# K, Q and x of a fused attention and MLP kernel turned in other ways, with the order of its work held as tables

## The chip, the cores and the metric

The kernel runs on one core of one Trainium2 chip. The metric is the time of one execution on the device in microseconds; the median of three runs is compared. A core has TensorE (PE; its weight loads are listed as PEld), VectorE (DVE), ScalarE (ACT), GpSimd (POOL) and SyncE (SP). DMAs are issued from the queues of SP, ACT and POOL and carried by 16 DMA engines.

## The reference

Causal attention in which each query sees only the best 6 of 24 chunks of 32 keys, followed by an MLP with ELU.

```python
B, H, S, D = 4, 8, 768, 64          # chunk = 32, nc = 24, top_k = 6
k_min, k_max = min and max of k over each chunk          # per head dimension
ub = sum over d of max(q * k_min, q * k_max)             # -1e9 where the chunk lies ahead
top_chunks = argsort(ub)[..., -6:]
scores = q @ k.T / sqrt(D);  scores = -1e9 outside the chosen chunks and above the diagonal
attn = softmax(scores);  o = attn @ v
x = o.transpose(0, 2, 1, 3).reshape(B * S, H * D)        # 3072 x 512
h = x @ w_in                                             # 3072 x 2048
out = where(h > 0, h, exp(min(h, 0)) - 1) @ w_out        # 3072 x 512
```

q, k and v have the shape (4, 8, 768, 64) in 32-bit floats; w_in is 512 x 2048, w_out 2048 x 512.

## The kernel before, in words

The unit of work is a pair of heads of one batch (16 pairs, `u` from 0 to 15, four to a batch), and within it a half of the 768 positions (`hf`, 384 each). The two heads of a pair lie on partitions 0 to 63 and 64 to 127.

For each pair K and Q must have the head dimension on partitions. In batches 1 to 3 (`pair_prep`, from L613) four DMAs a tensor bring K and Q in 128-byte pieces into `stage`, SP issues them (L623), and the DVE turns them in 32x32 blocks (L636, L654). In batch 0 (`first_prep`, from L670) sixteen loads of K and Q (one a pair, half and tensor; L706; the first two Qs from ACT's queue) bring four consecutive tokens of a head, 1 KB, to each of 96 partitions; they are kept in two `gT` buffers, `stage` and `kt`. V comes in sixteen DMAs (L712) in pieces of 256 bytes. TensorE turns a block (`turn`, L735): for each of the four tokens and both heads a 32-bit matmul of 96x64 against a 96x96 identity, written to a PSUM bank (psH for K, psMT for Q). Since the tokens come out in four interleaved groups, the copies that follow undo this: ScalarE's for K (L759), Q (L779) and relu(Q) (L784), and the DVE's chunk minima and maxima (L765).

Then, for two pairs together, `quad_sel` computes the chunks' bounds on TensorE (L833) and picks the best six on DVE (L850 to L873); POOL copies the result as mask rows below Q (L884). `pair_attend` computes scores (L925, triangle L931), exponentials on ScalarE (L952), the triangle on POOL (L971) and the product with V (L984); the DVE divides by the sum (L997, L1000) into `on`, 128 tokens x 3 blocks x 128 columns. TensorE turns `on` in three bf16 transposes (L1009) into a PSUM bank, ScalarE copies the bank to `xT` (L1012). This happens once for each pair and half, 32 times.

`mlp(b, hf)` multiplies the `xT` of a batch's four pairs by w_in in 16 blocks (L1034), applies ELU with ScalarE and DVE (L1044 to L1078), multiplies by w_out (L1097), copies (L1105) and stores from SP (L1109). It follows the attention of its batch by two or three pairs, so that TensorE always has dense work between the attention's steps.

The order is not written out: every operation is registered with an engine, a duration and a priority (`Plan.add`), and `Plan.order` simulates engines, DMA queues and buffers and lets each engine take the ready operation of least priority number. RANKS moves single priorities. The result is a sequence in which the operations are emitted, with a buffer slot for each tile. Each engine then executes its operations in that order.

Of the kernel before, what the change touches and what calls it, by code (L numbers as in the profile page):

```python
# [13 lines left out]
F32 = mybir.dt.float32  # L14
# [3 lines left out]
H = 8  # L18
# [24 lines left out]
def WHEN(q_in, left, out):  # L43
# [8 lines left out]
TURN = 0.7  # L52
FILL = {}
TWO = False
# [4 lines left out]
RANKS = ((0, 1, 127), (11, 1, 71), (17, 1, -43), (33, 1, -100), (37, 1, -51), (48, 1, 127), (49, 1, -12),  # L59
# [60 lines left out]


class Plan:

    LAT = {"PE": 0.21, "ACT": 0.17, "DVE": 0.13, "POOL": 0.08, "SP": 2.2, "POOLQ": 2.5}

    BEGIN = 0.85  # L130
    COLD = 7.0
    RING = 2560
    LANES = 8
# [1065 lines left out]
```

## Time and profile before

| | us |
|---|---|
| median of three runs (least, most) | 272.35 (272.06, 272.52) |
| span of the profiled execution, first to last instruction | 276.5 |
| TensorE busy in it | 266.1 (96%) |
| DVE, ScalarE, POOL busy | 198.8, 202.8, 124.5 |

No time is recorded for the profiled execution other than its span; the span is 4.15 us above the median of the runs. In the lists of instructions the columns are: start and duration (timeline) or count, busy time and mean of one (groups), the engine, the line of the kernel, the operation, the tile written and the tiles read, the form. "x16" is the number of instructions that the line stands for. Matmuls are pipelined: the distance between the starts of two neighbours is what one costs.

### The profile page before, as it was taken

What the parts mean: (1) busy time and instruction counts of PE and PEld (TensorE: products, weight loads), DVE (VectorE), ACT (ScalarE), POOL (GpSimd) and SP (SyncE); (2) the same over time, 40 slices, a digit from 0 to 9 for tenths busy, and PEclk for the clock granted to TensorE, in tenths of its full rate; (3) what the DMA queues carried; (4) which work ended last, traced back from release to release, by engine and by line L of the source; (5) the groups of instructions that cost most, each with busy time, mean ns of one, the idle gap of its engine ahead of it and who ended that gap; (6) DMA issues with size and microseconds to landing.
All of it is one profiled execution on the core that took longest, in us unless ns stands there. A gap on an engine that the chain in (4) does not pass through costs nothing.

```text
span 276.5 us, 6918 instructions
## 1 busy us (share of the span) xinstructions
PE 266.1 (96%) x2573; PEld 165.0 (60%) x2600; DVE 198.8 (72%) x526; ACT 202.8 (73%) x382; POOL 124.5 (45%) x219
## 2 busy tenths in 40 slices
PE   8889998899999999999999999999999999999995
PEld 4778855565555565655556565666556655555544
DVE  5944686995998998799699953876884846615920
ACT  2956799994797899988979989779579744435411
POOL 5783182794687499766537776010062200000000
PEclk9965899999999999999999999999999999999999
DMA  7999989499997999999974301101010111011022
GB/s 183 235 236 189 189 124 167 73 162 152 149 235 112 199 149 183 177 173 153 158 168 79 78 2 38 40 0 40 10 70 0 40 39 38 28 51 38 2 76 76
DMA packets 111473, 29.81 MB, mean 108 GB/s; under 512 B 101072, under 2 KB 108496, under 8 KB 111440
## 3 DMA queue, kind: packets, MB, share of 16 engines
q1 hardware_dynamic: 106800, 24.78, 48.2%
q0 software_dynamic: 4224, 4.19, 9.8%
q8 instruction: 20, 0.33, 0.5%
q10 hardware_dynamic: 416, 0.39, 0.5%
q14 instruction: 13, 0.11, 0.1%
HBM read 27.26 MB, written 6.29 MB: 121 GB/s over the span
## 4 chain that ended last, share of the span: by engine, by line
PE 71%; DMA 10%; DVE 5%; ACT 5%; issue 3%; SPq 2%; POOL 2%; ACTq 0%; DVEq 0%; POOLq 0%
PE psM L1097 17%; PE psH L1034 15%; PE psS L925 10%; PE psS L1034 8%; PE psMT L1097 7%; PE psO L984 6%; DMA gT<-in_q_dram 4%; DMA w_out_sb<-in_moe_w_out_dram 3%; ACT pt L952 2%; PE psS L833 2%; PE psT L1009 2%; PE psH L735 2%; DMA stage<-in_q_dram 2%; DMA stage<-in_k_dram 1%; SPq L712 1%
## 5 line engine op out<-in xcount | busy, mean ns | idle before, releaser
L952 ACT ACTIVATE pt<-psS 128x768 bf16<-128x768 f32 (+1 forms) x120 | 90.0, 788 | 9.1 <-PE psS L925 7.8
L1034 PE MATMUL psH<-xT,w_in_sb 128*128 128x384 bf16 x384 | 72.9, 325 | 0.1
L1097 PE MATMUL psM<-w_out_sb,gT 128*128 128x512 bf16 x264 | 68.2, 379 | 1.6 <-DMA w_out_sb<-in_moe_w_out_dram 0.2
L1034 PEld LDWEIGHTS <-w_in_sb 128*128 128x128 bf16 x512 | 48.2, 97 | 32.8 <-issue 0.9
L971 POOL TENSOR_SCALAR_AFFINE_SELECT pt<-pt 128x256 bf16<-128x256 bf16 (+1 forms) x56 | 28.8, 518 | 65.5 <-ACT pt L952 64.2
L925 PE MATMUL psS<-rhs,lhs 88*128 88x384 bf16 (+4 forms) x304 | 55.3, 292 | 1.6 <-ACT pt L952 0.7
L1097 PEld LDWEIGHTS <-gT 128*128 128x128 bf16 x400 | 37.1, 97 | 33.0 <-issue 1.2
L1044 ACT ACTIVATE e<-psH 128x384 f32<-128x384 f32 x96 | 47.0, 513 | 8.9 <-PE psH L1034 7.2
L925 PEld LDWEIGHTS <-lhs 88*128 88x128 bf16 x304 | 28.8, 101 | 17.0 <-issue 2.5
L984 PEld LDWEIGHTS <-pt 128*128 128x128 bf16 x672 | 28.5, 99 | 9.6 <-issue 1.7
L1073 DVE SCALAR_TENSOR_TENSOR t<-e,psH 128x384 bf16<-128x384 f32 x48 | 25.5, 545 | 12.1 <-ACT e L1044 11.9
L801 POOL CAST rhs<-qt 64x768 bf16<-64x768 f32 (+1 forms) x40 | 27.9, 701 | 13.3 <-ACT qt L779 11.5
L884 POOL COPY rhs<-selt 24x576 bf16<-24x576 bf16 (+2 forms) x40 | 22.6, 564 | 25.0 <-DVE selt L873 23.3
L984 PE MATMUL psO<-vext,pt 128*128 128x65 bf16 x672 | 32.1, 196 | 0.3 <-POOL pt L971 0.2
L1052 DVE SCALAR_TENSOR_TENSOR gT<-e,psH 128x384 bf16<-128x384 f32 x48 | 25.3, 540 | 9.7 <-ACT psH L1049 9.6
L1044 ACT ACTIVATE e<-psS 128x768 f32<-128x768 f32 x16 | 13.0, 810 | 18.4 <-PE psS L1034 18.4
L1078 DVE SCALAR_TENSOR_TENSOR gT<-psH,t 128x384 bf16<-128x384 f32 x48 | 25.5, 545 | 0.5
L1049 ACT ACTIVATE psH<-psH 128x384 f32<-128x384 f32 x48 | 24.5, 522 | 0.0
L801 POOL CAST lhs<-kt 64x768 bf16<-64x768 f32 x24 | 19.9, 831 | 6.7 <-DVE kt L636 4.5
L1034 PE MATMUL psS<-xT,w_in_sb 128*128 128x384 bf16 x128 | 22.4, 326 | 0.0
L1097 PE MATMUL psMT<-w_out_sb,gT 128*128 128x512 bf16 (+1 forms) x109 | 22.1, 348 | 0.2
L1012 ACT ACTIVATE xT<-psT 128x384 bf16<-128x384 bf16 x32 | 15.8, 501 | 8.6 <-PE psT L1009 8.5
(66 smaller groups left out, 287.6 us busy)
## 6 DMA issues: line engine op xcount, KB each, us to landing
out_dram<-osb SPq DMA_DIRECT2D x23, 256.0 KB, 2.0
stage<-in_k_dram SPq DMA_DIRECT2D x48, 96.0 KB, 3.6
stage<-in_q_dram SPq DMA_DIRECT2D x48, 96.0 KB, 3.8
vd<-in_v_dram SPq DMA_DIRECT2D x12, 384.0 KB, 4.7
w_in_sb<-in_moe_w_in_dram POOLq DMA_DIRECT2D x4, 512.0 KB, 8.4
w_out_sb<-in_moe_w_out_dram POOLq DMA_DIRECT2D x4, 512.0 KB, 9.5
gT<-in_v_dram SPq DMA_DIRECT2D x16, 96.0 KB, 5.1
gT<-in_k_dram SPq DMA_DIRECT2D x6, 192.0 KB, 5.0
```

What stands on the lines that cost most here:

```text
L801: nc.gpsimd.tensor_copy(out=o, in_=i)
L925: nc.tensor.matmul(p_s[:, hd, pc:pc + w], lhsT=tiles[pt_["kb"]][0:64 + NCH, hd, 128 * kb:128 * kb + 128], rhs=tiles[pt_["qb"]][0:64 + NCH, ...
L952: lambda bs=bs, pt=pt, wtot=wtot, lo=lo, at=at: nc.scalar.activation(out=tiles[pt][:, :, lo:lo + wtot], in_=tiles[bs[0]][:, :, at:at + wto ...
L971: nc.gpsimd.affine_select(out=a, in_=a, compare_op=AOT.is_ge, fill=0.0, base=0, pattern=pat, channel_multiplier=-1)
L984: nc.tensor.matmul(po[:, hd, qi, :], lhsT=tiles[pt][:, hd, off:off + 128], rhs=tiles[pt_["vx"]][:, 6 * hd + kb, :], start=(kb == 0), stop= ...
L1034: nc.tensor.matmul(ph, lhsT=w_in_sb[:, kk, f0:f0 + 128], rhs=tiles[XT[4 * b + kk]][:, c0:c0 + HALF], start=(kk == 0), stop=(kk == NKK - 1))
L1044: lambda e=e, view=view: nc.scalar.activation(out=tiles[e][:, 0:step], in_=view(), func=AF.Exp),
L1049: lambda view=view: nc.scalar.activation(out=view(), in_=view(), func=AF.Relu),
L1052: lambda e=e, view=view, fc=fc, gt=gt: nc.vector.scalar_tensor_tensor(out=tiles[gt][:, fc:fc + step, :], in0=tiles[e][:, 0:step], scalar=1 ...
L1073: lambda e=e, t=t, view=view: nc.vector.scalar_tensor_tensor(out=tiles[t][:, 0:step], in0=tiles[e][:, 0:step], scalar=1.0, in1=view(), op0 ...
L1078: lambda t=t, view=view, fc=fc, gt=gt: nc.vector.scalar_tensor_tensor(out=tiles[gt][:, fc:fc + step, :], in0=view(), scalar=0.0, in1=tiles ...
L1097: nc.tensor.matmul(pm, lhsT=tiles[gt][:, fc, 128 * tt:128 * tt + 128], rhs=w_out_sb[:, fc, cs], start=(fc == 0), stop=(fc == NFC - 1))
```

## The change

Four things are changed.

- **Loads of batch 0.** K and Q of four heads come in one load of three DMAs, one for each block of 128 tokens: a token to a partition, four heads of 64 numbers (256 bytes each) beside each other. There are eight such loads instead of sixteen. V of all eight heads comes in one load of three DMAs a half. All are staged in three `gT` buffers.
- **Turns of batch 0.** A block of 128 tokens by two heads (128x128, 32 bits) is turned by one `nc.tensor.transpose`; three make a turn. The tokens come out in order, so the copies and reductions read the bank straight.
- **Turns of x in batches 1 to 3.** `on` goes to `xT` by a transposing DMA issued by SP, 24 in all; the three transposes on TensorE and ScalarE's copy are not made there. Batch 0 keeps them.
- **The order.** `Plan.order` no longer simulates; it reads the operations' numbers from ORDER and the slots from SLOTS. RANKS and the constants of the simulation are gone.

```diff
+XDMA = (False, True, True, True)
-TURN = 0.7
+TURN = 0.40
+VLATE = 2.2
...
-RANKS = ((0, 1, 127), (11, 1, 71), (17, 1, -43), (33, 1, -100), (37, 1, -51), (48, 1, 127), (49, 1, -12),
...
+ORDER = (
+    0, 3, 13, 15, 6, 1, 43, 2, 4, 10, 45, 8, 7, 5, 9, 25, 11, 19, 26, 153, 12, 31, 20, 37, 28, 32, 47, 29, 21, 155,
+    33, 80, 22, 38, 59, 34, 48, 40, 23, 27, 60, 41, 17, 53, 35, 49, 24, 39, 36, 50, 61, 71, 54, 51, 81, 65, 56, 183,
...
+    1308, 1568, 1589, 1314, 1590, 1569, 1591, 1315, 1574, 1592, 1318, 1570, 1575, 1511, 1571, 1319, 1512, 1572,
+    1556, 1557, 1513, 1558, 1514, 1576, 1560, 1593, 1515, 1561, 1562, 1516, 1563, 1517, 1585, 1594, 1316, 1595,
+    1518, 1520, 1586, 1596, 1521, 1519, 1522, 1577, 1523, 1524, 1525, 1320, 1578, 1309, 1321, 1579, 1580, 1581,
+    1587, 1618, 1588, 1582, 1583, 1597, 1619, 1622, 1620, 1584, 1598, 1623, 1630, 1322, 1624, 1621, 1323, 1604,
...
     def order(self):
-        ops = self.ops
...
+        left = iter(SLOTS)
+        return [(self.ops[i], [(h, next(left)) for h in self.ops[i].alloc]) for i in ORDER]
...
+        def load(h, at, src, h0, w, eng):
             def f():
...
+                for n in range(3):
+                    eng.dma_start(out=tiles[h][:, at, n, :].rearrange("p (h d) -> p h d", d=D),
+                                  in_=src[a + P * n:a + P * n + P, h0:h0 + w])
             return f
...
+        if j == 0:
+            early = hf == 0 and g == 0
+            fetch(1.5, pl, load(sh, 2 * g, kb0, 4 * g, 4, nc.sync), [(sh, 2 * g)], (0.0185, 1536, 3), alloc=[] if g else [sh])
+            fetch(1.5, pl + 0.1, load(sh, 2 * g + 1, qb0, 4 * g, 4, nc.scalar if early else nc.sync), [(sh, 2 * g + 1)],
+                  (0.0185, 1536, 3), eng="ACT" if early else "SP")
+            if not g:
+                fetch(1.5, pl + VLATE, load(sv, hf, vb0, 0, 8, nc.sync), [(sv, hf)], (0.0185, 3072, 3), alloc=[] if hf else [sv])
...
-                for j in range(4):
-                    for hd in range(2):
-                        x0 = 256 * hd + 64 * j
-                        nc.tensor.matmul(p_[64 * hd:64 * hd + 64, 96 * j:96 * j + 96], lhsT=at()[0:96, x0:x0 + 64],
-                                         rhs=ident_f[0:96, 0:96], start=True, stop=True)
+                for n in range(3):
+                    nc.tensor.transpose(p_[:, P * n:P * n + P], tiles[sh][:, i, n, P * j:P * j + P], ident_f)
             return f
...
+            if XDMA[u // 4]:
+                uid[0] += 1
+                w = ("turned", uid[0])
+                o = add("SP", 0.5, pr,
+                        lambda on=on, hf=hf: nc.sync.dma_start_transpose(
+                            out=tiles[xt_h][:, HALF * hf:HALF * hf + HALF].rearrange("p (n t) -> p n t", n=3),
+                            in_=tiles[on].rearrange("p n h d -> p (n h d)")),
+                        reads=[on], writes=[w, (xt_h, hf)], alloc=[] if hf else [xt_h], lat=0.0)
+                add("DMA", 0.0, 0.0, lambda: None, reads=[w], writes=[(xt_h, hf)], free=[on], lat=2.0,
+                    dma=("SP", 0.03, 384, 1), issues=o)
+                return
```

The numbers in ORDER count the operations as they are registered. For the steps that are named later: 1517 to 1522 are the products with V of pair 14, second half, 1523 and 1524 the DVE's division, 1525 its transposing DMA; 1563 is that of pair 15; 1577 and 1581 are up-projections of batch 3's first half (eight matmuls each), 1320 and 1321 down-projections of batch 2 (four each); 1618 is the first up-projection of batch 3's second half.

More of the change, by code (lines that the diff above doesn't have):

```diff
@@ L187, in order @@
     def order(self):
-        ops = self.ops
-        for first, n, shift in RANKS:
-            for o in ops[first:first + n]:
-                o.prio += 0.02 * shift
-        for o in ops:
-            o.left = len(o.deps) + len(o.after)
-            o.ready = 0.0
-            o.start = o.end = None
-            for d in o.deps:
-                d.users.append(o)
-            for d in o.after:
-                d.followers.append(o)
-        free_slots = {c: [(0.0, i) for i in range(n)] for c, n in self.caps.items()}
@@ L234, in order @@
-        waiting = {}
-        for o in ops:
-            if o.eng == "DMA":
-                continue
-            waiting.setdefault(o.eng, [])
-            engines[o.eng] = self.BEGIN
-            if not o.left:
-                waiting[o.eng].append(o)
-        n_left = sum(o.eng != "DMA" for o in ops)
-        port = {"POOL": 0.0, "DVE": 0.0}
-        out = []
-        parts = {}
-        stalls = []
-        taken, asked = 2 * WARM, self.FETCH[0]
-        queues = {"SP": [], "ACT": [], "POOL": []}
@@ L739, in fill @@
-        def fill(i, bb, done):
-            n = FILL.get((u - SPLIT[0], hf, i), 0)
-            if not n:
-                return False
-            def f():
-                for _ in range(n):
-                    nc.tensor.matmul(ps(bb, [P, HALF], F32), lhsT=blank[:, 0:P], rhs=blank[:, 0:HALF], start=True, stop=True)
-            add("PE", 0.163 * n, pr - 0.01, f, reads=["blank"], writes=[done], alloc=bb, ni=2 * n)
-            return True
-        def tok(x):
-            return x.rearrange("q (j p) -> q p j", j=4)
@@ L754, in first_prep @@
[L754 to L756 removed]
+                for n in range(3):
+                    nc.tensor.transpose(p_[:, P * n:P * n + P], tiles[sh][:, i, n, P * j:P * j + P], ident_f)
+            return f
+        add("PE", TURN, pr, turn(bk, 2 * g), reads=[(sh, 2 * g), "ident"], writes=[bk[0]], alloc=bk, ni=6)
@@ L1154 @@
     steps = plan.order()
-    if DUMP is not None:
-        DUMP(steps)
     with tc.manual_schedule():
```

273 lines of the change are left out of this document (24 added, 249 removed), and 158 rows, old and new, of tables (ORDER, RANKS, SLOTS).

## The prediction

> **What bounds the kernel now.** I read the page's first two parts and the chain, to find the engine that sets the time.
>
> ```profile
> span 276.5 us, 6918 instructions
> PE 266.1 (96%) x2573; PEld 165.0 (60%) x2600; DVE 198.8 (72%) x526; ACT 202.8 (73%) x382; POOL 124.5 (45%) x219
> ...
> PEclk9965899999999999999999999999999999999999
> ...
> PE 71%; DMA 10%; DVE 5%; ACT 5%; issue 3%; SPq 2%; POOL 2%; ACTq 0%; DVEq 0%; POOLq 0%
> ```
>
> TensorE is busy for 96% of the span and carries 71% of the chain; the next engines stand at 72 and 73%. The clock row has one hole: from the third slice to the fifth (13.8 to 34.6 us) the granted clock falls. The windows show when each thing binds (columns: length, busy time of PE, PEld, DVE, ACT and POOL, then granted clock, DMA share, GB/s).
>
> ```profile
> 7.00:13.00 6.00, 5.04 (x134) 4.50 (x128) 5.55 (x13) 5.58 (x14) 4.59 (x9) 1.00 1.24 238
> 13.00:20.00 7.00, 5.98 (x97) 5.03 (x98) 4.08 (x26) 3.96 (x13) 5.84 (x13) 0.73 1.17 233
> 20.00:30.00 10.00, 10.00 (x110) 8.91 (x107) 3.71 (x10) 6.46 (x13) 3.55 (x8) 0.51 0.96 186
> ...
> 50.00:70.00 20.00, 18.96 (x213) 11.70 (x215) 17.18 (x49) 16.16 (x31) 14.67 (x24) 1.00 0.95 141
> ...
> 90.00:110.00 20.00, 19.59 (x190) 12.12 (x191) 18.77 (x44) 17.85 (x30) 15.71 (x26) 1.00 1.14 177
> 110.00:130.00 20.00, 19.83 (x177) 11.64 (x178) 18.07 (x52) 17.42 (x39) 14.07 (x22) 1.00 0.96 169
> ...
> 150.00:170.00 20.00, 19.78 (x208) 11.97 (x211) 13.62 (x44) 18.18 (x32) 16.30 (x26) 1.00 0.20 48
> ```
>
> Three stretches: a head to about 35 us, in which loads run at 230 GB/s and TensorE gets half its clock while it is 100% busy; a middle to 150 us in which both TensorE (98 to 99%) and the DMA engines (share near 1) are full; and the rest, in which the DMA share is 0.2 or less and only TensorE is full. So an instruction taken off TensorE shortens the run by its own length, as long as what feeds the next matmul keeps up. The whole idle time of TensorE is 276.5 - 266.1 = 10.4 us; there is little else to win.
>
> **Turns of x.** The change takes the turns of batches 1 to 3 off TensorE and ScalarE and gives them to SP as transposing DMAs.
>
> ```profile
> L1012 ACT ACTIVATE xT<-psT 128x384 bf16<-128x384 bf16 x32 | 15.8, 501 | 8.6 <-PE psT L1009 8.5
> ...
> L1009 PE MATMUL psT<-ident_b,on 128*128 128x128 bf16 x96 | 10.8, 222 | 0.8 <-DVE on L1000 0.8
> ```
> ```profile
> 30.10 0.33 PE L1009 MATMUL psT<-ident_b,on 128*128 128x128 bf16 x3
> 30.26 0.44 PE L984 MATMUL psO<-vext,pt 128*128 128x65 bf16 x9
> ...
> 31.59 0.34 PE L1009 MATMUL psT<-ident_b,on 128*128 128x128 bf16 x3
> 31.77 0.41 PE L984 MATMUL psO<-vext,pt 128*128 128x65 bf16 x8
> ```
>
> 96 matmuls are 32 turns of three; 24 of them go. One holds TensorE from its start to the next group's start: 0.16 and 0.18 us, so 24 x 0.17 = 4.1 us, all at full clock and nearly all in stretches where TensorE is full. I count it whole. ScalarE loses 24 x 0.50 = 12 us; at 73% it does not bind, so I count nothing for it, nor for the PSUM bank that each turn held.
>
> **Turns of K and Q.** Before, a turn is eight 32-bit matmuls, seen as 16 records; after, three 128x128 ones. There are 16 turns.
>
> ```profile
> 6.03 0.83 PE L735 MATMUL psMT<-ident_f,gT 96*64 96x96 f32 x16
> 6.69 0.83 PE L735 MATMUL psH<-ident_f,gT 96*64 96x96 f32 x16
> ...
> 21.46 1.55 PE L735 MATMUL psH<-ident_f,gT 96*64 96x96 f32 x16
> 22.94 0.29 PE L984 MATMUL psO<-vext,pt 128*128 128x65 bf16 x2
> ```
>
> Start to start, 0.66 us at full clock and 1.48 at half. No row shows a 32-bit 128x128 transpose. From below: three bf16 ones take 0.17. From above: if the two heads of a pair now overlap in the array, 768 columns in 0.66 us hide another 768, a column costs 1.72 ns alone, and 3 x 128 columns cost 0.66, no gain. I take what 384 columns cost at the row's own 0.86 ns: 0.33 us. So 16 x (0.66 - 0.33) = 5.3 us at full clock (0 to 7.8). About five turns stand in the half-clock stretch and save as much again: 5 x 0.33 = 1.65. Sum 6.9 us. The cover that this needs: TensorE must have other work ready; with 10.00 busy of 10 at 20 to 30 us it has.
>
> The copies out of PSUM change from interleaved to contiguous reads; a 64x384 copy took 483 ns and a contiguous 128x384 one 513, so nothing is counted.
>
> ```profile
> L1044 ACT ACTIVATE e<-psH 128x384 f32<-128x384 f32 x96 | 47.0, 513 | 8.9 <-PE psH L1034 7.2 <-DVE gT L1052 1.0
> L759 ACT ACTIVATE lhs<-psH 64x384 bf16<-64x384 f32 x16 | 7.7, 483 | 6.4 <-PE psH L735 6.2
> ```
>
> **Loads of batch 0.** K and Q come in eight loads of 384 KB (three DMAs each) instead of sixteen of 192 KB, in pieces of 256 bytes instead of 1 KB; V, in 256-byte pieces before too, in two loads behind the K and Q of the first heads.
>
> ```profile
> 4.79 1.41 PE L735 MATMUL psH<-ident_f,gT 96*64 96x96 f32 x16
> ...
> 8.66 0.88 PE L735 MATMUL psH<-ident_f,gT 96*64 96x96 f32 x16 [0.49 <-DMA gT<-in_k_dram]
> ```
>
> Now the first turn starts at 4.79 us, the second pair's K (the turn at 6.69) two turns later. After, the first turn needs what the first two pairs needed, so it starts near 6.7; but four turns then follow at 0.33 and end at 8.0, before the third pair's turn started at 8.66. ScalarE begins later by some 1.5 us; half of the head's cost of that is taken back by turns that come together. I take +1.0 us (0 to +3). The loads issue on SP and ACT without waits; behind them on ACT's queue stands only its table load.
>
> A rule of the Trainium skill speaks against it: "DMA: Bandwidth & Descriptors", section Specifications, gives 512 bytes as the least piece for line rate, below which a read-modify-write is made. The head's rows, with V in 256-byte pieces among the loads, hold 233 to 238 GB/s; the middle's, mostly 128-byte pieces, 141 to 177. By that rule K and Q would run like the middle; it is priced as a rival below.
>
> **The transposing DMAs.** Each moves 96 KB, waits on SP for the DVE's `on`, and behind it on SP stand the K, Q and V loads of the next pairs, for which the DVE's 32x32 transposes wait, and the stores of the output, whose buffers ScalarE's copies take next.
>
> ```profile
> out_dram<-osb SPq DMA_DIRECT2D x23, 256.0 KB, 2.0
> stage<-in_k_dram SPq DMA_DIRECT2D x48, 96.0 KB, 3.6
> ...
> stage<-in_q_dram SPq DMA_DIRECT2D x1, 192.0 KB, 9.4
> ```
> ```profile
> 244.50 0.86 PE L984 MATMUL psO<-vext,pt 128*128 128x65 bf16 x22
> 245.21 1.89 PE L1097 MATMUL psMT<-w_out_sb,gT 128*128 128x512 bf16 x7
> 246.93 0.33 PE L1009 MATMUL psT<-ident_b,on 128*128 128x128 bf16 x3
> 247.10 1.03 PE L1097 MATMUL psMT<-w_out_sb,gT 128*128 128x512 bf16 x4
> 247.96 2.76 PE L1034 MATMUL psS<-xT,w_in_sb 128*128 128x384 bf16 x16
> ```
>
> No transposing DMA is in the trace. By size the nearest row is the 96 KB load, 3.6 us; the quickest is 2.0, the slowest 9.4. When the last x falls due the DMA engines are nearly idle, so I take 3. The tightest hand-off is the last. In the new order there stand on TensorE, between the last product with V of batch 3 (entry 1522) and the first matmul that needs its x (1618), entries 1577, 1320, 1321 and 1581: two times eight matmuls of 384 columns (half of the 2.6 us that the sixteen from 247.96 occupy, 1.3 each) and two times four of 512 (0.86 each, 247.10 to 247.96), 4.3 us in all. The DVE needs about 1 us for the division, which leaves 3.3 for issue and landing. I take 0.5 us lost over all hand-offs (0 to 18, below). For batch 1 the cover is similar: scores, products with V and two groups of four down-matmuls. The DMA engines' extra 24 x 96 KB = 2.4 MB are, at 141 to 177 GB/s, 14 to 17 us of transfer; a third of it falls where their share is near 1, and K and Q of batch 2 come that much later, some 5 us. That batch's loads are asked for well ahead and DMA is idle from 150 us on; nothing counted.
>
> **The clock.** The hole, closer:
>
> ```profile
> 15.00:16.00 1.00, 0.84 (x17) 1.00 1.19 235
> 16.00:17.00 1.00, 1.00 (x26) 0.58 1.25 214
> ...
> 29.00:30.00 1.00, 1.00 (x16) 0.60 1.23 210
> 30.00:31.00 1.00, 1.00 (x37) 1.00 1.23 203
> ```
>
> From about 16.2 to 29.8 us, 13.6 us at half clock, worth 6.8 us of full-clock work. I leave it as it is: the new head has the same kind of small matmuls and the same waits around 12 to 15 us.
>
> **Sum.** -4.1 (x) - 6.9 (K and Q) + 1.0 (head) + 0.5 (hand-offs) = -9.5 us: span 276.5 to 267.0. The span of this profile is 4.15 us above the median of the runs, 272.35; I carry that difference over unchanged: **262.9 us**.
>
> **Rivals.**
> 1. The clock stays low longer. The hole opened although TensorE was then busy all the time, so it is not busy time alone that opens the gate; the new turns may count for even less. Shut from the first turn (6.7) to the first dense matmuls (34.67 before, some 32 after), 25 us instead of 13.6: up to 5.7 us more, 268.6. For it: 100% busy at 0.50 for 13 us. Against: fewer such matmuls.
>
> ```profile
> 34.67 3.42 PE L1034 MATMUL psH<-xT,w_in_sb 128*128 128x384 bf16 x20
> ```
>
> "TensorE: Matmul & The Clock Gate", Part 4, in the Trainium skill says the same: transpose mode does not count as busy time for the gate. No transpose-mode matmul with 32 bits is in this trace to agree or not.
> 2. The gate does not shut: the head's waits of 12 to 15 us vanish with the earlier turns; 6.8 us less where TensorE binds, of which 5 are felt: 257.9.
> 3. The head hangs on its loads: 3.15 MB of K and Q at 141 instead of 235 GB/s is 22.3 instead of 13.4 us, 8.9 us more, of which the gain of the turns hides some 4: about 268. Against: V's pieces did not slow the head.
> 4. The turns do not get cheaper (0.66 each): 262.9 + 6.9 = 269.8.
> 5. **Slower**: the transposing DMA lands late. At 9.4 us, the slowest row, each hand-off that has 3.3 us of cover stalls 6.1; with three such (first of batch 1, both of batch 3) 18 us, less the 0.5 counted: 280. It outweighs the gain of 10 once three stalls make 10, that is from a landing of 3.3 + 3.3 = 6.6 us. For it: SP is one ordered queue on which the turn stands among loads. Against: at the last hand-off no load is left.
> 6. The gain is eaten: stalls of the new order and DMA contention in the middle give back 8 to 11 us: 271 to 274.
>
> **Chances.** Forecast 0.46 (259 to 266), rival 1 0.12, 2 0.08, 3 0.06, 4 0.08, 5 0.13, 6 0.07. Rivals 1 to 4 and the forecast are faster: 0.80. Rival 6 is split, 0.03 within 0.2% (about what a measurement of this kernel can tell from no change) and 0.02 each side; with 5, slower 0.15, same 0.03, faster 0.82. The range takes in the forecast and rivals 1 to 4, from 256.5 to 270.5 us; outside are 5 and 6, 0.20.
>
> **What would show it.** TensorE's busy time near 256 us, still over 95% of the span; turns of three records at about 0.33 us; 24 transposes in the DMA table landing within 3 us or so; first up-projection before 34.67 us. The forecast is wrong if TensorE's idle time grows past 15 us, with waits on xT's DMA ahead of the up-projection, or if the clock row has a longer hole.

## The result and the profile after

The changed kernel takes 271.2 us (median of 20 runs, 269.7 to 272.6). Against the kernel before, run beside it on the same chip, the ratio is 0.995 with a 95% interval of [0.9933, 0.9967]: 0.5% faster, some 1.4 us, where 262.9 was forecast and 270.5 was the upper end of the range. In some executions of the kernel before, the profiled one of the prediction among them, TensorE ran at half clock for some 13 us; they take about 277.5 us instead of 272 and are left out of all ratios here. So the kernel before is shown here by a second profile, taken in the first experiment, in which the clock stayed up (execution 271.75 us, span 270.0; for the changed kernel 271.61 and 269.9).

The page of the changed kernel, and below it the same rows of the kernel before with its clock up:

```profile
span 269.9 us, 6328 instructions
PE 253.0 (94%) x2295; PEld 151.5 (56%) x2320; DVE 200.3 (74%) x526; ACT 192.0 (71%) x358; POOL 123.7 (46%) x219
...
q1 hardware_dynamic: 124800, 27.15, 59.2%
...
PE 66%; DMA 13%; DVE 9%; ACT 3%; issue 2%; SPq 2%; POOL 2%; ACTq 0%; DVEq 0%; POOLq 0%
```
```profile
span 270.0 us, 6945 instructions
PE 261.6 (97%) x2600; PEld 159.8 (59%) x2600; DVE 199.1 (74%) x526; ACT 202.6 (75%) x382; POOL 124.8 (46%) x219
...
q1 hardware_dynamic: 106800, 24.78, 49.2%
...
PE 76%; ACT 10%; DMA 4%; DVE 4%; issue 2%; POOL 2%; SPq 1%; ACTq 0%; DVEq 0%; POOLq 0%
```

By these rows TensorE's busy time fell by 8.6 us and its idle time grew from 270.0 - 261.6 = 8.4 us to 16.9. Some 1.3 us of that are a gap in the record: the changed kernel's page has 2295 matmuls beside 2320 weight loads, so 25 matmuls are missing (all down-projections), and each leaves a hole of about 0.05 us in work that ran on. So about 7.3 us came off TensorE, where 4.1 + 5.3 were forecast, its idle time is nearer 15.6 us, and the span stayed. In the chain, TensorE went from 76 to 66%, DMA from 4 to 13%. The question is why 7.3 us taken off the engine with the most work became about as much waiting. The windows show where (columns as before: length, busy time of PE, PEld, DVE, ACT, POOL, clock, DMA share, GB/s); first after, then before:

```profile
13.00:20.00 7.00, 5.34 (x95) 4.39 (x93) 5.36 (x29) 6.90 (x20) 5.78 (x13) 1.00 1.26 186
20.00:30.00 10.00, 7.64 (x129) 5.99 (x130) 8.33 (x34) 9.60 (x23) 5.70 (x12) 1.00 1.23 221
...
50.00:70.00 20.00, 17.95 (x169) 10.01 (x170) 16.22 (x45) 13.05 (x26) 12.51 (x19) 1.00 1.18 176
...
130.00:150.00 20.00, 18.64 (x170) 10.64 (x171) 19.12 (x53) 16.43 (x31) 14.22 (x23) 1.00 1.08 156
```
```profile
13.00:20.00 7.00, 6.39 (x132) 5.50 (x134) 5.13 (x28) 5.87 (x17) 6.48 (x14) 1.00 1.13 234
20.00:30.00 10.00, 9.57 (x196) 7.79 (x192) 7.65 (x33) 9.33 (x21) 4.37 (x9) 1.00 1.22 223
...
50.00:70.00 20.00, 20.00 (x195) 11.73 (x194) 17.51 (x50) 15.27 (x30) 13.43 (x21) 1.00 1.05 158
...
130.00:150.00 20.00, 20.00 (x237) 11.80 (x235) 18.37 (x54) 18.23 (x36) 13.50 (x22) 1.00 0.70 125
```

From 20 to 30 us TensorE idles 2.36 us (0.43 before), from 50 to 70 it idles 2.05 (0), from 130 to 150 1.36 (0). What it waits for is not one thing. The waits of TensorE in the changed kernel (waiting line, releaser: us in all, times, longest):

```profile
PE psS L709 <- ACT pt L736: 1.7, 3, 0.8
PE nothing L955 <- DVE blank L953: 1.3, 1, 1.3
PE psH L829 <- DMA w_in_sb<-in_moe_w_in_dram: 1.2, 1, 1.2
PE psMT L541 <- DMA gT<-in_q_dram: 1.1, 2, 0.8
PE psM L892 <- DMA w_out_sb<-in_moe_w_out_dram: 0.9, 1, 0.9
```

The wait on `blank` is there before too. The others are exponentials, the loads of Q, and both weights. Nobody on TensorE waits for a transposing DMA, though the up-projections read what they write. The rows of that DMA (the issue on SP; least, median and most) and the time from issue to landing:

```profile
L792 SPq DMA_TRANSPOSE xT<-on x24: 1178/1221/2724, 85.9 to 231.9; - x24
...
DMA to landing us min/median/max: 2.3/2.5/6.1
```

### The profile page after: what moved, and what is told of

The parts are those of the page before. It is cut to its first block, busy times and chain, and to the rows that moved or that the text cites. A ratio compares the mean times of both kernels' runs of the same rounds, so it can differ in the third digit from the quotient of the medians.

```text
span 269.9 us, 6328 instructions
## 1 busy us (share of the span) xinstructions
PE 253.0 (94%) x2295; PEld 151.5 (56%) x2320; DVE 200.3 (74%) x526; ACT 192.0 (71%) x358; POOL 123.7 (46%) x219
## 3 DMA queue, kind: packets, MB, share of 16 engines
q1 hardware_dynamic: 124800, 27.15, 59.2%
## 4 chain that ended last, share of the span: by engine, by line
PE 66%; DMA 13%; DVE 9%; ACT 3%; issue 2%; SPq 2%; POOL 2%; ACTq 0%; DVEq 0%; POOLq 0%
PE psM L892 18%; PE psH L829 17%; PE psS L709 9%; PE psS L829 8%; PE psMT L892 8%; PE psO L768 5%; DMA w_in_sb<-in_moe_w_in_dram 4%; DMA stage<-in_k_dram 3%; DMA vd<-in_v_dram 2%; DMA gT<-in_q_dram 2%; DMA stage<-in_q_dram 1%; SPq L455 1%; POOL rhs L668 1%; ACT lhs L547 1%; DVE gT L847 1%
## 5 line engine op out<-in xcount | busy, mean ns | idle before, releaser
L736 ACT ACTIVATE pt<-psS 128x768 bf16<-128x768 f32 (+2 forms) x120 | 89.1, 781 | 18.5 <-PE psS L709 16.6
L829 PE MATMUL psH<-xT,w_in_sb 128*128 128x384 bf16 x384 | 73.9, 325 | 2.8 <-DMA w_in_sb<-in_moe_w_in_dram 1.2
L829 PEld LDWEIGHTS <-w_in_sb 128*128 128x128 bf16 x512 | 47.4, 97 | 36.7 <-issue 4.0
L839 ACT ACTIVATE e<-psH 128x384 f32<-128x384 f32 x96 | 46.3, 505 | 14.5 <-PE psH L829 13.5
L709 PE MATMUL psS<-rhs,lhs 88*128 88x384 bf16 (+4 forms) x304 | 54.0, 283 | 1.8 <-ACT pt L736 1.7
L768 PEld LDWEIGHTS <-pt 128*128 128x128 bf16 x672 | 32.0, 98 | 13.9 <-ACT pt L736 1.4
L768 PE MATMUL psO<-vext,pt 128*128 128x65 bf16 x672 | 36.9, 194 | 1.6 <-DVE rc L781 0.6
L709 PEld LDWEIGHTS <-lhs 88*128 88x128 bf16 x304 | 26.8, 98 | 14.3 <-issue 2.1
L857 DVE TENSOR_SCALAR t<-e 128x768 bf16<-128x768 f32 x16 | 8.8, 558 | 16.3 <-ACT e L839 16.3
```

The lines of the kernel that those rows point to most:

```text
L709: nc.tensor.matmul(p_s[:, hd, pc:pc + w], lhsT=tiles[pt_["kb"]][0:64 + NCH, hd, 128 * kb:128 * kb + 128], rhs=tiles[pt_["qb"]][0:64 + NCH, ...
L736: lambda bs=bs, pt=pt, wtot=wtot, lo=lo, at=at: nc.scalar.activation(out=tiles[pt][:, :, lo:lo + wtot], in_=tiles[bs[0]][:, :, at:at + wto ...
L768: nc.tensor.matmul(po[:, hd, qi, :], lhsT=tiles[pt][:, hd, off:off + 128], rhs=tiles[pt_["vx"]][:, 6 * hd + kb, :], start=(kb == 0), stop= ...
L829: nc.tensor.matmul(ph, lhsT=w_in_sb[:, kk, f0:f0 + 128], rhs=tiles[XT[4 * b + kk]][:, c0:c0 + HALF], start=(kk == 0), stop=(kk == NKK - 1))
L839: lambda e=e, view=view: nc.scalar.activation(out=tiles[e][:, 0:step], in_=view(), func=AF.Exp),
```

## The experiments

The theory that the traces suggest: the turns' time was saved where TensorE was not what the next step waited for, so it turned into waiting. Its rivals: the time had worth and was eaten, by the short pieces of the loads, by ScalarE, or by an order that does not suit the operations. Ratios are to the kernel before, run beside each kernel on the same chip; where two experiments are compared, their ratios are. 0.1% is 0.27 us.

**The offset of the profile.** The prediction set its sum against a span 4.15 us above the median. The kernel before, with no edit at all:

> The kernel before, unchanged. Its 20 runs fall into two groups, about 272 and 277.5 us, and the profile that the prediction was made from (span 276.5, clock 0.974) has a hole of 13.6 us at half clock. Theory A, the hole is the second group: runs near 277.5 show a mean granted clock near 0.97 and runs near 272 one of 0.99 or more; a profile of the 272 kind has no hole and TensorE busy near 260 us instead of 266. Theory B, the two groups have another cause: the clocks of both groups are alike and a profile of the 272 kind has the hole too.

But for two (274.9 us at 1.0 and 276.1 at 0.981), the runs came in two groups: 271.65 to 273.5 us at a mean granted clock of 0.998 to 1.0, and 277.5 to 278.1 at 0.973 to 0.975; the prediction's profile has 0.974. Time is span + 1.7 in both. The offset was the clock hole, and nothing that one carries over.

**The size of the turns, and where their time has worth.** Three runs put TensorE's time back into the changed kernel, and nothing else. First the turns of batch 0 as 32-bit matmuls:

```diff
-nc.tensor.transpose(p_[:, P * n:P * n + P], tiles[sh][:, i, n, P * j:P * j + P], ident_f)
+nc.tensor.matmul(p_[:, P * n:P * n + P], lhsT=tiles[sh][:, i, n, P * j:P * j + P], rhs=ident_f,
+                 start=True, stop=True)
```

> The changed kernel with one thing undone: each 128x128 block of batch 0's K and Q is turned by a 32-bit matmul against the identity in place of the transpose (48 of them, the same order, buffers and loads). If a turn of three then costs about 0.66 us as the eight small matmuls did before, TensorE's busy time rises by 16 x 0.33 = 5.3 us. Theory H (the time that the cheaper turns save is not worth anything in this head, because the turns wait for loads and ScalarE and the next matmuls wait for w_in): 271 us, within 1.5 us of the changed kernel, and TensorE's idle time falls by about what its busy time gains. Theory W (TensorE's time is worth its full length there, and the gain was lost elsewhere): 274.5 to 277. If the turn costs 0.33 as a matmul too, neither is told and the transpose was no cheaper than the matmul.

Then the turns of x, by matmuls of zeros:

```diff
+if u >= 4 and hd == 1 and qi == 2:
+    for _ in range(5):
+        nc.tensor.matmul(po[:, hd, qi, :], lhsT=blank[:, 0:P], rhs=blank[:, 0:D + 1], start=True, stop=True)
```

> The changed kernel with TensorE's time for the turns of x put back: in pairs 4 to 15, ahead of the last product with V of each half, five matmuls of 65 columns of zeros against zeros, which the product then overwrites (24 x 5, some 0.17 us a half, 4 us in all). The transposing DMAs stay. Theory H (where the order leaves TensorE waiting, its time has no worth; the pairs of batch 1, to 110 us, wait): TensorE's idle time takes back up to half, +1.5 to +3 us. Theory W (whole worth): +4 us, 275.

Then both edits at once:

```diff
+    nc.tensor.matmul(p_[:, P * n:P * n + P], ...
...
+    for _ in range(5):
+        nc.tensor.matmul(po[:, hd, qi, :], lhsT=blank[:, 0:P], ...
```

> Both at once: the changed order, loads and transposing DMAs with TensorE's time as it was before the change (some 9 us more busy time). Theory H: 272.5 to 275. Theory W: 278 to 281. If the two single runs add up here, the stretches do not touch each other.

| | TensorE busy, us | span | ratio to before |
|---|---|---|---|
| changed kernel | 253.0 (25 records missing; some 254.3 with them) | 269.9 | 0.9950 [0.9933, 0.9967] |
| + K and Q time | 258.0 | 268.7 | 0.9935 [0.9897, 0.9972] |
| + x time | 257.0 | 270.0 | 0.9989 [0.9961, 1.0017] |
| + both | 262.0 | 272.6 | 1.0056 [1.0016, 1.0097] |

The rows of the turns, as matmuls and as transposes (start and duration; the distance of two starts is what a turn costs):

```profile
13.00 0.94 PE L541 MATMUL psMT<-ident_f,gT 128*128 128x128 f32 x6
13.77 0.83 PE L541 MATMUL psH<-ident_f,gT 128*128 128x128 f32 x6
14.44 0.25 PE L710 MATMUL psS<-rhs,lhs 88*128 88x192 bf16 x1
```
```profile
8.21 0.85 PE L541 MATMUL psMT<-ident_f,gT 128*128 128x128 f32 x3
8.85 0.85 PE L541 MATMUL psH<-ident_f,gT 128*128 128x128 f32 x3
9.49 0.37 PE L709 MATMUL psS<-rhs,lhs 88*128 88x192 bf16 x1
...
14.84 0.52 PE L541 MATMUL psH<-ident_f,gT 128*128 128x128 f32 x3
15.19 0.82 PE L541 MATMUL psMT<-ident_f,gT 128*128 128x128 f32 x6
```

A turn by matmuls costs 0.67 us (13.77 to 14.44), by transposes 0.35 (14.84 to 15.19) once the first ones, at 0.64, are past: the 0.33 of the prediction was nearly right for twelve of the sixteen. Sixteen at 0.67 make 10.7 us, twelve at 0.35 and four at 0.64 make 6.8, so the head saves some 3.9 us by it. They have no worth that can be seen: with them put back the kernel is no slower (0.9935 beside 0.9950; by the two intervals, at most about 0.7 us slower). The x time, 24 times 0.16 us from start to start, is 3.8 us and has 0.4%, 1.1 us. Both together, some 7.7 us, cost 1.06%, 2.9 us (1.7 to 4.1 by the intervals); that is more than the two singly, so they draw on the same slack. Where it was, the busy time up to 50 us and after shows (window, length, busy), for the changed kernel, with the K and Q time, and with both, in this order:

```profile
0.00:50.00 50.00, 41.73 (x495) 1.00 1.12 178
50.00:270.00 220.00, 211.30 (x1805) 1.00 0.61 106
```
```profile
0.00:50.00 50.00, 44.66 (x527) 1.00 1.11 174
50.00:270.00 220.00, 213.34 (x1843) 1.00 0.60 107
```
```profile
0.00:50.00 50.00, 45.19 (x519) 1.00 1.08 170
50.00:270.00 220.00, 216.84 (x1969) 1.00 0.56 106
```

Up to 50 us the changed kernel's TensorE is busy for 41.7 us and has 8.3 to spare. With the K and Q time back, it is busy for 2.9 us more by that point, in time that was idle. Behind 50 us the two rows differ by 2.0 us, of which 1.3 are the missing records, which all lie there.

This gives the whole sum. With TensorE's time as it was, the rest of the change (short pieces, transposing DMAs, the new order) makes the kernel 0.56% slower than before, +1.5 us; the 7.7 us of TensorE give back 2.9; together -1.4. How the 1.5 us divide among pieces, DMAs and order, these three runs do not tell.

**The loads.** K and Q of batches 1 to 3 in pieces of 3 KB, in the changed kernel and in the kernel before; K, Q and V of batch 0 in pieces of 1 to 2 KB; and all of them in the changed kernel. The long pieces bring as many bytes to the same tiles, but from the wrong places, so these kernels compute wrong numbers and serve as probes only.

```diff
-nc.sync.dma_start(out=tiles[h][r0:r0 + 32, :].rearrange("c (m i) -> c m i", i=32), in_=src[2 * u + hd, e])
+nc.sync.dma_start(out=tiles[h][r0:r0 + 32, :], in_=src[2 * u + hd, e])
```

> The changed kernel, but K and Q of batches 1 to 3 are loaded in pieces of 3 KB instead of 128 bytes: the same bytes to the same buffers in the wrong arrangement, so what is computed from batch 1 on is not the reference's. It takes most of the loads' time off the DMA engines (77 us of each engine's time go to the 128-byte pieces). Theory A, the saved TensorE time is now spent waiting for what the loads feed: 4 to 6 us faster, 265 to 267, and TensorE's idle time falls from 16.9 to 12 us or less. Theory C, the waits belong to the new order itself (ScalarE, DVE and TensorE waiting for each other): within 1 us of 271.2.

> The kernel before with the same longer pieces for K and Q of batches 1 to 3 (same bytes in the wrong arrangement). Theory A, before the change the loads bind less: 0 to 2 us faster than 272.3, so that with long pieces the two kernels differ by 5 us or more, near the 7.9 that the prediction's TensorE terms make without the head. Theory C: within 1 us of 272.3, and the two kernels differ by about 1 us with long pieces too.

```diff
-eng.dma_start(out=tiles[h][:, at, n, :].rearrange("p (h d) -> p h d", d=D),
-              in_=src[a + P * n:a + P * n + P, h0:h0 + w])
+flat = src[0, h0:h0 + w].rearrange("h (r m) d -> (h r) (m d)", m=w)
+r = 3 * P * hf + P * n
+eng.dma_start(out=tiles[h][:, at, n, :], in_=flat[r:r + P])
```

> The changed kernel with K, Q and V of batch 0 loaded in pieces of 1 KB and 2 KB instead of 256 bytes: the same bytes to the same buffers in the wrong arrangement, so batch 0 is not the reference's. Theory E (the short pieces make the head's loads and the first w_in late; TensorE idles 7.5 us before 30 us, 4.1 more than before the change): 2 to 4 us faster than the changed kernel's 271.2. Theory D (ScalarE is the full engine from 13 to 50 us whatever the loads do): at most 1 us faster.

> The changed kernel with long pieces everywhere: K, Q and V of batch 0, and K and Q of batches 1 to 3 (same bytes in the wrong arrangement, so nothing is the reference's). If the loads are what turns the saved TensorE time into idle time (theories A and E): 265 to 267, with TensorE's idle time at 11 us or less, near the 8.4 that the kernel before has in a profile without the clock hole. If the order itself does it (theory C): 269 or more, idle 14 us or more.

Measured: later batches alone 0.9932 [0.9908, 0.9955] (270.05 us), the head alone 0.9904 [0.9884, 0.9924] (269.4), all 0.992 [0.9895, 0.9946] (270.17); the kernel before 1.0056 [1.0038, 1.0075], not faster but slower, and why is not known. So the pieces of the head cost 0.46%, 1.3 us (0.6 to 2.0 by the intervals; between what the two theories had said), those of the middle 0.2%, inside the intervals, and both together no more than one. V's pieces of 256 bytes, which the kernel before has too, are part of the 1.3. The wait from 130 to 150 us goes, as the rows from 90 to 150 us show (long pieces in batches 1 to 3, then the changed kernel), but the one from 50 to 70 stays (17.95 of 20 in the changed kernel), and the time with it:

```profile
50.00:70.00 20.00, 17.86 (x175) 10.16 (x174) 16.40 (x46) 13.14 (x25) 12.47 (x20) 1.00 0.94 195
...
90.00:150.00 60.00, 59.86 (x600) 35.73 (x597) 55.62 (x150) 53.22 (x100) 43.74 (x69) 1.00 0.62 152
```
```profile
90.00:150.00 60.00, 57.81 (x562) 34.05 (x567) 54.47 (x148) 51.79 (x98) 41.54 (x66) 1.00 1.03 154
```

The DMA engines were relieved to 0.62, TensorE idles some 2 us less there, and the kernel gains less than that.

K and Q of batch 0 now come in pieces of 256 bytes, and from 13 to 20 us 186 GB/s are moved, 234 before. The price of 1.3 us is a seventh of the 8.9 us of transfer at which rival 3 put it. "DMA: Bandwidth & Descriptors" of the Trainium skill, section Specifications, puts the limit for line rate at 512 bytes. These runs agree with it in direction.

**ScalarE and w_out.** ScalarE is busy for 36.1 of the 37 us from 13 to 50 in the changed kernel (6.90, 9.60, 9.62 and 10.00 in the windows), though its share of the span is 71%. Eight of its copies were given to VectorE; in another run, w_out, for which TensorE waits 0.9 us, is asked for earlier in POOL's order.

```diff
-add("ACT", act(HALF), pr,
-    lambda hd=hd: nc.scalar.activation(out=tiles[kb][0:64, hd, a:b], ...
+add("DVE" if hd else "ACT", act(HALF), pr,
+    lambda hd=hd: nc.vector.tensor_copy(out=tiles[kb][0:64, hd, a:b], in_=ps(bk, None, None)[64:128, :]) if hd
```

> The changed kernel with the copies of the second head's K of batch 0 (8 of 483 ns, 3.9 us) made by the DVE instead of ScalarE, at the same places of the order. Theory D (ScalarE binds the head): 1 to 3 us faster than 271.2. Theory E (the loads bind the head) : within 0.7 us of 271.2, or slower where the DVE is now late for something.

```diff
 ORDER: 327 moved from entry 308 to 225, 329 from 324 to 251, 331 from 331 to 282, 333 from 344 to 311
```

> The changed kernel with the four loads of w_out issued earlier in POOL's order (by about 12, 8, 5 and 3 us). In the changed kernel they are issued at 44 to 48.5 us and land 7.7 to 11.7 us later; TensorE idles 2.05 us between 50 and 70 us, in the kernel before (issued at 33.6 and 48.6 us) not at all. Theory F (those 2 us are the wait for w_out): 1 to 2 us faster than 271.2. Rival (the DMA engines are full at 30 to 50 us, so the pairs' loads lose what w_out gains): within 0.7 us.

The copies: 0.9964 [0.9939, 0.9988], nothing gained. The earlier w_out: 1.008 [1.0052, 1.0108], 1.3% slower than the changed kernel. Its windows:

```profile
40.00:50.00 10.00, 9.42 (x107) 6.30 (x105) 8.63 (x17) 10.00 (x20) 5.63 (x11) 1.00 1.34 200
50.00:70.00 20.00, 15.04 (x148) 8.26 (x148) 13.45 (x40) 9.13 (x18) 8.53 (x14) 0.91 0.87 118
```

The DMA share goes to 1.34 (0.92 in the changed kernel), and from 50 to 70 us all engines have less to do (the clock of 0.91 is taken up below). The waits between 48 and 70 us tell why: VectorE waits 6.0 us at once for a Q, and TensorE 4.6 for the gT that VectorE, standing there in order, has not made.

```profile
DVE qt L475 <- DMA stage<-in_q_dram: 6.0, 1, 6.0
...
PE psH L818 <- DVE gT L862: 4.6, 1, 4.6
```

**Both at once.** If loads and ScalarE stood side by side, either alone would hide behind the other.

```diff
+flat = src[0, h0:h0 + w].rearrange("h (r m) d -> (h r) (m d)", m=w)
...
+add("DVE" if hd else "ACT", act(HALF), pr,
```

> The changed kernel with K, Q and V of all batches in pieces of 1 to 3 KB (the same bytes to the same tiles from wrong places, so the numbers mean nothing) and, in addition, eight of the sixteen K copies of batch 0 moved from ScalarE to VectorE. Theory J (loads and ScalarE stand side by side as what the head waits for, so that either alone leaves the other): both together give clearly more than the loads alone (270.2), 265 to 268. Theory O (the waits are built into the order: each engine waits in turn for the next at the place that the table gives): 269 to 271, no more than the loads alone.

```diff
+nc.tensor.matmul(p_[:, P * n:P * n + P], lhsT=tiles[sh][:, i, n, P * j:P * j + P], rhs=ident_f,
```

> The kernel of the run beside it (long pieces, K copies shared with VectorE), with the turns of batch 0 as 32-bit matmuls against the identity again, 5 us more of TensorE's time. Theory J: with the loads and ScalarE relieved, TensorE's time in the head has worth, +3 to +5 us on that run. Theory O: within 1 us of it.

They do not: 0.9945 [0.9914, 0.9977] (270.68 us). With 5.4 us of TensorE's time put back on top, 0.9984 [0.9961, 1.0007] (271.44 us): 0.8 us by the medians, 1.1 by the ratios, far from 3 to 5. The window from 50 to 70 us of the first of them still has its wait, and TensorE's waits name what ended it:

```profile
50.00:70.00 20.00, 17.88 (x163) 9.89 (x163) 15.12 (x44) 11.87 (x24) 11.56 (x18) 0.91 0.86 179
```
```profile
PE psM L894 <- DMA w_out_sb<-in_moe_w_out_dram: 2.0, 1, 2.0
```

With what comes ahead of it relieved, TensorE waits for w_out 2.0 us instead of 0.9. The clock of 0.91 in the row comes on top: the wait ends at 59.0 us, and from 60 to 64 us the granted clock is 0.59, 0.50, 0.50 and 0.70, which is 1.7 us of full-clock work. The run with w_out early shows the same behind its 4.6 us (0.72, 0.50, 0.50 and 0.57 from 57 to 61 us); the changed kernel, with its 0.9 us of waiting there, shows 1.00. So in this profile a late w_out costs about 3.7 us, nearly twice its wait, and may hide part of what the long pieces give. The weight is issued from 43.99 us on, from 44.04 in the changed kernel: at its place in POOL's order, whatever else got quicker. So the last run gives w_out and w_in earlier places in that kernel too:

```diff
 ORDER: 321 moved from entry 115 to 99, 323 from 173 to 116, 325 from 224 to 174, 327 from 308 to 225,
        329 from 324 to 251, 331 from 331 to 282, 333 from 344 to 311
```

> The kernel with long pieces in all batches and the K copies shared with VectorE (270.7 us; its loads come from wrong places, so the numbers mean nothing), with one more edit: the issues of w_in and w_out stand earlier in POOL's order (w_in's second, third and fourth quarter where the first, second and third stood or right behind; w_out's from where w_in's last stood). In the changed kernel and in that kernel alike, the second quarter of w_in is issued at 19.7 us and the up-projections run on from 29.5; w_out is issued from 44.0 on. Theory P (the weights' places in POOL's order set the head, which is why nothing else that was relieved had worth): up-projections run on from about 27 us, TensorE's waits for both weights vanish, 266 to 268.5 us. Theory S (no single wait sets it; relieving one lets the next come up): 269.5 to 272, TensorE's idle time of 50 to 70 us moving to another releaser.

It took 267.36 us, 0.982 [0.9793, 0.9847]: 1.25% less than without the edit, 3.4 us, and the fastest time of this study, though of a probe. The waits for both weights are gone from TensorE's list, and the window from 50 to 70 us is full and at full clock:

```profile
30.00:50.00 20.00, 18.60 (x191) 11.46 (x190) 17.93 (x50) 19.91 (x40) 13.48 (x26) 1.00 0.88 143
50.00:70.00 20.00, 19.84 (x193) 11.59 (x195) 18.80 (x49) 15.63 (x30) 14.01 (x22) 1.00 0.60 149
```

The up-projections still run on from 29.42 us (29.45 without the edit), not from 27 as the theory had it. So of the two weights w_out, issued from 33.78 us on, ten us earlier, is the likely cause: its wait and the clock behind it made some 3.7 us, the wait for w_in 0.6. It was not moved alone in this kernel. The same move of w_out in the changed kernel cost 1.3%. The difference lies most likely in the DMA engines: there the early w_out found them at a share of 1.03 from 30 to 50 us, and held up K and Q; here at 0.50, and raised it to 0.88. So neither the short pieces nor w_out's place shows its price alone: with short pieces there is no room to ask for w_out earlier, and with w_out late the room that long pieces make is worth little.

**The order.** Four kernels with the planner of the kernel before in place of the tables, all with RANKS cut short (its later entries belong to operation numbers that the change shifts): nothing else changed, the transposing DMAs alone, batch 0 alone, both.

```diff
-          (962, 1, 84), (969, 1, 122), (970, 1, 112), (973, 1, 122), (974, 1, -57), (993, 1, 110),
...
-          (1575, 1, -74), (1577, 1, -43), (1580, 1, -34), (1583, 1, -23), (1586, 1, -64))
```

> The kernel before, with its planner, but only the part of RANKS that moves operations below number 1000 (with the rest, the planner finds no order once x is turned by DMA); the base of a square of four kernels that take the two parts of the change apart, each with an order of its own from the planner. All theories: within 3 us of the kernel before (272.3 without the clock hole).

> The base plus the transposing DMAs for x of batches 1 to 3 alone. Theory A (the DMAs cost the loads what TensorE saves): within 1 us of the base. Theory B (the 4.1 us of TensorE time are gained, since TensorE is the full engine from 30 us on and the loads do not bind before): 3 to 4.5 us under the base.

> The base plus the new loads and turns of batch 0 alone. Theory D (in the head ScalarE is the full engine: 36.1 of the 37 us from 13 to 50 us in the changed kernel, and 256-byte pieces make the weights land later, so TensorE time saved there is idle time): between 2 us faster and 1.5 us slower than the base. Theory B (TensorE time is gained wherever it is saved): 4 us or more under the base.

> Both parts, ordered by the planner instead of the tables. If the parts add up: the sum of the two differences to the base. Theory C (the tables cost what the parts gain): under the 271.2 us of the changed kernel by 2 us or more, at 269 or less. If the tables are the better order, as much above it.

Measured: 1.0144 [1.0102, 1.0185], with the DMAs 1.0263 [1.0212, 1.0314], with batch 0 1.0398 [1.0349, 1.0447], with both 1.0434 [1.0409, 1.0458]. The base itself is 1.4% slower than the kernel before, 3.9 us where at most 3 were expected. By the planner each part makes the kernel slower than that base, by 1.2 (from two runs), 2.5 and 2.9%, though TensorE has less to do. With both parts the clock was down in all six runs (a mean of 0.976 to 0.982; in the profile 0.61, 0.85 and 0.83 in the windows from 7 to 13, 20 and 30 us, some 5 us of full-clock work), while the base's ratio is from runs at 1.0. The same operations by the tables stand at 0.995: the tables are worth up to 4.8%, some 13 us, to the changed operations, of which up to 5 may be the clock. One row at full clock shows that not all of it is, planner with both parts and planner alone:

```profile
110.00:150.00 40.00, 33.97 (x313) 19.20 (x297) 37.92 (x101) 28.97 (x61) 23.21 (x36) 1.00 1.02 156
```
```profile
110.00:150.00 40.00, 38.85 (x343) 23.11 (x342) 36.76 (x100) 36.22 (x75) 26.88 (x42) 1.00 0.89 144
```

TensorE idles 6 us of 40 instead of 1.2, with the clock up. In these kernels the order, and not only the operations, decides what is gained.

Last, one that failed as a test: the changed order with x turned on TensorE and ScalarE again, at the places of SP's DMAs.

```diff
-XDMA = (False, True, True, True)
+XDMA = (False, False, False, False)
...
+            for t in list(turns):
+                x = bank()
```

> The changed kernel and its order, but x of batches 1 to 3 is turned by TensorE and copied by ScalarE again (24 turns), each at the place at which SP issued the transposing DMA. Theory A, the transposing DMAs cost about what they save, since they slow and delay the loads of the pairs while the DMA engines are full: the time is within 1.5 us of the changed kernel's 271.2. Theory B, the 4.1 us taken off TensorE are gained whole and something else eats the rest: 4 us slower, about 275.

It took 284.21 us, 1.0453 [1.0436, 1.047], a number of neither theory. The order has no free PSUM bank laid out for these turns, and what follows waits for ScalarE to empty them:

```profile
PE psH L870 <- ACT xT L848: 2.4, 5, 0.6
PE psT L845 <- ACT xT L848: 2.2, 5, 0.6
```

It says nothing of TensorE's time, only shows that the bank and ScalarE's copy, which the prediction counted at nothing, do cost where there is no room for them. The matmuls of zeros above were made to avoid this.

## Why the prediction was wrong, point by point

- **Turns of x, 24 x 0.17 = 4.1 us:** the size holds (3.8 put back), the worth does not: 1.1 us alone.
- **Turns of K and Q, 5.3 us:** the size is some 3.9, because four turns cost 0.64 instead of 0.33; the worth is 0, to within some 0.7 us. The further 1.65 us for turns at half clock belong to the 13 us hole, which neither the runs of before in the ratio nor the changed kernel have.
- **The failed step** is the sentence "an instruction taken off TensorE shortens the run by its own length, as long as what feeds the next matmul keeps up", with the cover named for it: "with 10.00 busy of 10 at 20 to 30 us it has". That row was taken in the clock hole. At half clock (0.51 in that row) the same work fills more of TensorE's time; with the clock up the same window reads 9.57, and 40 to 50 us 8.59 of 10:

```profile
40.00:50.00 10.00, 8.59 (x78) 5.02 (x76) 9.94 (x33) 9.38 (x18) 5.19 (x9) 1.00 1.00 158
```

  Of the middle, too, the prediction says 98 to 99%, where its own row from 50 to 70 us has 18.96 of 20, 95%. The head was no longer TensorE's. Of some 7.7 us, 2.9 have worth.
- **"ScalarE at 73% does not bind":** a share of the whole span; from 13 to 50 us it is full. Yet relieving it gave nothing, so it is not what the head waits for alone.
- **Loads of batch 0, +1.0:** the first full turn starts near 6.9 us, as forecast (6.7). The four turns that should end at 8.0 end at 9.5, because the first cost 0.64 each. The short pieces cost 1.3 in all. The weights were not looked at: the first up-projection starts at 27.51 us, does one block and waits for w_in until 29.50. The 34.67 that it was to come before was taken in the clock hole; with the clock up the kernel before runs on from 29.02 without a wait, so the dense work comes no earlier than it did. In the timeline of before, and in the chain of waits of the changed kernel:

```profile
29.02 3.42 PE L1034 MATMUL psH<-xT,w_in_sb 128*128 128x384 bf16 x20
```
```profile
19.73 9.72 DMA w_in_sb<-in_moe_w_in_dram
29.50 2.12 PE psH L829 x12
```

  w_in lands 9.72 us after its issue, among the loads of batch 1.
- **Transposing DMAs:** landing 3 us was assumed, 2.5 is the median; no matmul waits for one, so rival 5 falls. "Nothing counted" for their transfer was too little in the middle: the queue of the loads has 59.2% of 269.9 us instead of 49.2% of 270.0, 27 us more on each DMA engine, K and Q's shorter pieces among it; relieving it (long pieces) took some 2 us of waiting out of 90 to 150 us, but not out of the time.
- **The offset of 4.15 us, carried over:** it was the hole. On a base without it the terms (-4.1 - 5.3 + 1.0 + 0.5 = -7.9) give 272.35 - 7.9 = 264.45. The bookkeeping thus made 1.6 us of the miss. The other 6.8 us are TensorE's time: of the 9.4 us in these terms some 1.7 were not saved, and some 4.8 of the 7.7 saved have no worth. The costs beside it came to 1.5 us, as much as the 1.0 + 0.5 of the sum. That is luck as far as is known: the head's pieces may make most of it (1.3, not measured in that kernel), and the transposing DMAs were not told apart.
- **Rival 6**, the gain eaten by stalls of the new order and contention, 271 to 274 us, is the one whose number came. It had 0.07. Its mechanism is not quite the one found: the stalls and the contention cost about what the forecast had allowed; most of the gain was never there, because TensorE has slack in the head and in the middle, where its time was not what the next step waited for. Of the others, rival 2 had its condition right, since the long clock hole did not come, but not its price: it had 5 us of that time felt. Rival 1's longer hole did not come, and rival 4 falls by the 0.35 us of a turn.

**What stays open.** Shown is that much of the turns' time had no worth (2.9 of 7.7 us had it, 1.7 to 4.1 by the intervals), that relieving loads or ScalarE gives little with w_out where it is, and that both weights early, with long pieces, give 3.4 us. Whether TensorE's time in the head would have its full worth in that last kernel was not tried, so what holds the head before 50 us (TensorE is busy for 39.4 of these 50 us there) is not settled: the waits left are many and short. The price of the transposing DMAs by themselves, in the tables' order, was not measured cleanly.

## What to carry to other kernels

Busy 96% of the span does not make an engine's time worth its length everywhere: before counting a saving, read the windows of the stretch where it falls, in a profile whose clock matches the runs that it is set against. To learn what a saving is worth, put the time back into the changed kernel with idle work and look whether it gets slower; that took three runs here and settled what relieving one suspect after another had not. And an order fixed by hand or by tables belongs to the durations that it was made for: when the operations change, part of the gain lies in the order.

## What the hardware showed

- A turn of three 128x128 32-bit blocks costs 0.35 us as transposes and 0.67 as matmuls against the identity, but the ones between 6.9 and 9.5 us of the changed kernel's profile cost 0.64 as transposes too, with a granted clock of 1.00 in that window. In the run with the x time put back the first two cost 0.33 (six records from 6.89 to 7.54); then the granted clock falls, to 0.50 from 8 to 9 us, and a turn costs 0.64 (8.06 to 8.70, the start of the next matmul):

```profile
6.89 0.82 PE L541 MATMUL psH<-ident_f,gT 128*128 128x128 f32 x6
7.54 0.73 PE L541 MATMUL psMT<-ident_f,gT 128*128 128x128 f32 x3
8.06 0.85 PE L541 MATMUL psH<-ident_f,gT 128*128 128x128 f32 x3
```
```profile
8.00:9.00 1.00, 1.00 (x8) 0.50 1.39 218
```

  So 0.64 is the price at half clock in that run, and the changed kernel's slow turns look alike, though the record says 1.00. Turns by matmuls can be slow in the same place: in the run with both times back the first two take 2.56 us (7.20 to 9.76) instead of 1.34, at a recorded 1.00 too. "TensorE: Matmul & The Clock Gate" of the Trainium skill, Part 4, says that transpose mode does not engage full clock as other matmuls do. No run here sets the two apart: both kinds are seen at either price.
- In 12 of the 20 runs of the changed kernel the mean granted clock is 0.987 to 0.994, which is 3 to 7 us at half clock; they are no slower than the other eight (medians 271.1 and 271.4 us). In the profile of the run with the x time put back (a mean of 0.994) the hole lies in the head, where TensorE's time had no worth that can be seen.
- A transposing DMA of 128x384 bf16 holds SP for 1.22 us (median), and lands 2.3 to 6.1 us after issue beside loads at a DMA share above 1.
- Asking for a load earlier can slow a kernel: 2 MB of w_out, 4 to 12 us earlier, cost 3.2 us by the medians, with the half clock behind the wait, where the DMA engines were full (a share of 1.03 from 30 to 50 us), and in a kernel whose loads left them room (0.50) the early weights gained 3.3.
